# Attention and mixture of experts in one kernel: norm factors in a work bank, routing two periods sooner, token records in two tensors

## The chip, the cores and the metric

The kernel runs on one core of a Trainium2 chip. The metric is the device time of one execution in microseconds (us), lower is better. The engines are TensorE (PE, whose weight loads are listed apart as PEld), VectorE (DVE), ScalarE (ACT), GpSimd (POOL) and SyncE (SP), which here only starts transfers (DMAs).

## The reference

Eight batches of 12 heads, 448 positions, head size 64, all in float32. First attention with normalised q and k, then a mixture of eight experts beside a dense feed-forward network (FFN) on the 3584 tokens:

```python
q_n, k_n = rmsnorm(q, g_q), rmsnorm(k, g_k)        # over the 64 elements of a head
attn = softmax(q_n @ k_n.T / 8) @ v
x = attn.transpose(0, 2, 1, 3).reshape(3584, 768)  # tokens x (heads * 64)

h_dense = np.maximum(x @ w1_dense, 0.0)            # 768 -> 512
y_dense = h_dense @ w2_dense                       # 512 -> 768
logits = x @ w_gate                                # 768 -> 8
expert_idx = np.argmax(logits, axis=1)
gate_w = softmax(logits)[token, expert_idx]
for e in range(8):
    mask = expert_idx == e
    h = np.maximum(x[mask] @ w1[e], 0.0)
    y_moe[mask] = gate_w[mask, None] * (h @ w2[e])
out = y_dense + y_moe
```

## The kernel before, in words

**Attention stage.** It is cut into 24 periods `g` of four heads (two pairs of heads); three periods make a batch, `b, gb = divmod(g, 3)`. A period has seven steps `i`. In each step PE makes the scores of the next period's group for one of seven blocks of keys (`scores`, into the two double banks of PSUM pool `a_sc`), and ACT takes their exponential into SBUF (L285). In steps 1 and 2 PE multiplies the exponentials of this period with the values for the first of each pair's two heads (`attend`, head half 0, into the PSUM tile `av`), in steps 4 and 5 for the second (half 1). A column of ones beside the values gives the sums of the softmax; `divide` on DVE divides by them and writes tokens by features to `xa`.

Beside that, each period prepares later ones: `squares` (POOL) and `sums` (DVE) make the sums of squares for group g+3, `norms` (ACT: a logarithm, then two exponentials) makes the factors `rq` and `r`, `normalise` multiplies q (DVE) and k (POOL) with them into `xn`, `transposes` (PE) turns group g+2 into a work bank and `turned` (DVE) copies it out as `y`. In the kernel before, `rq` lies in unused columns of the tile `av`, and `norms` stands at the end of step 6, after `divide(g, 1)`.

**Work for the second half, woven in.** `xtrans` turns `xa` of group g-2 on PE into a work bank, `xturned` copies it to `xT` on DVE. With a whole batch in `xT`, `logits` (PE) makes the gate's logits, `choose` (DVE) picks the expert, `ranks` (PE) counts tokens per expert, `places` (DVE) finds each token's place and the selection matrices `sel`, `gates` (ACT, DVE) makes the softmax weight. `fill` gives PE dense matmuls of x with w1_dense, six in a group (`ff`), which ACT's `relu` empties. The work banks are the two banks of PSUM pool `a_wk`: each call takes the next of them, and the first instruction that writes a bank waits for the last that used it:

```python
ps = trs[name] = wkp.tile([P, J, P], BF16, tag="wk", name="tr")
R = wkp.tile([P, 512], F32, tag="wk", name="R")
ff[0] = wkp.tile([P, F], F32, tag="wk", name="ff")
```

**Records.** For each token the DRAM tensor `records` keeps 656 floats' worth: x in bf16 (384), the relu of the dense layer h (256), and the gate (16). `store` writes the parts from SP.

**The tail.** The last period (L619 to L656) is written out: attention of the last group, the rest of the routing, the rest of the dense groups, and `tables`, in which DVE works out from all counts which token lies in which slot, PE sums it up (`slp`, L448) and DVE writes the index table `row`.

**Expert stage.** The tokens are sorted into 32 to 35 tiles of 128 slots with one expert each. POOL gathers the records of a tile through `row` (`gather`, an indirect DMA, five tiles ahead). The first five tiles are turned on PE (`turn_here`, x and h apart, through one PSUM tile `xp`), later ones by transposing DMAs from SP (`turn`). Then `gemm1` (six matmuls, expert's w1), relu with the gate on ACT, `htrans`, and `gemm2`: eight matmuls of h with w2_dense and eight of the expert's w2 into the same PSUM tiles, two copies out (DVE, ACT) and an indirect DMA from POOL that scatters the tile to `out`.

The order of instructions on each engine is that of the program (`manual_schedule` over all five engines in the first half, over PE, POOL and SP in the second); engines run on their own and wait for each other through semaphores. An engine that waits holds up all that stands behind the waiting instruction.

Of the kernel before, what the change touches and what calls it, by code (L numbers as in the profile page):

```python
# [9 lines left out]
F32 = mybir.dt.float32  # L10
# [9 lines left out]
def kernel(  # L20
# [55 lines left out]
    XH = Dm // 2  # L76
    GO = XH + F // 2
    RC = GO + 16
# [21 lines left out]
    rec = nc.dram_tensor("records", (N, RC), F32).ap()  # L100
# [36 lines left out]
    def late_weight(i):  # L137

        o, w = wjobs[i]
        if i % 2:  # L140
            nc.gpsimd.dma_start(o, w, max_dma_last_dim=4 * Dm)
        else:
            nc.gpsimd.dma_start(o, w)
# [6 lines left out]
    with tc.tile_pool(name="a_ld", bufs=2) as ld, \  # L150
# [6 lines left out]


        av = avp.tile([P, GP, 512], F32, name="av")
        SP0 = 4 * De  # L160
        rq = av[:, 0, SP0:SP0 + 2 * J].rearrange("p (h j) -> p h j", h=2)
# [22 lines left out]
        gt = late[:, o:o + 8 * (RC - GO)].bitcast(F32).rearrange("p (m w) -> p m w", m=4)  # L184
        o += 8 * (RC - GO)
# [51 lines left out]
        def norms(g):  # L237
# [4 lines left out]
            rs["q"] = rq  # L242
# [88 lines left out]
        def store(b, lo, hi, x, chunks=range(4)):  # L331

            o = rec[b * S:(b + 1) * S].rearrange("(p u) w -> p u w", u=J)
            c = [m for m in chunks if m < 3]
            for hh in range(2):
                if c:
                    u = 2 * c[0] + hh
                    nc.sync.dma_start(o[:, u:u + 2 * len(c) - 1:2, lo:hi],
                                      x[hh * D:(hh + 1) * D, :len(c)])
            if 3 in chunks:  # L340
                nc.sync.dma_start(o[:, J - 1:, lo:hi], x[D:, len(c):])
# [26 lines left out]
        def gates(b, gt=gt):  # L368
# [4 lines left out]
            store(b, GO, RC, gt)  # L373
# [35 lines left out]
        def tables():  # L409
# [26 lines left out]
            slp = wkp.tile([P, NTL], F32, tag="wk", name="slp")  # L436
            for c in range(2):
# [9 lines left out]
                for n in range(c0, c1):  # L447
                    nc.tensor.matmul(slp, sel[:, n // 4, n % 4], val[:, :, n],  # L448
                                     start=(n == 0), stop=(n == NC4 - 1))

# [28 lines left out]
        def relu():  # L479
            while relus:  # L480
# [6 lines left out]
                store(b, XH, GO, hd.bitcast(F32).unsqueeze(1), [m])  # L487
# [6 lines left out]
        def period(g):  # L494
            b, gb = divmod(g, NB)
            for i in range(J):
                if i == 6:
                    divide(g, 1)
# [4 lines left out]
                if i == 0:  # L503
                    if g > 1:
                        xtrans(g - 2)
                    squares(g + 3, "k")
                    sums(g + 3, "q")
                if i == 5:
                    if gb == 0 and b > 1:
                        ranks(b - 2)  # L510
                        places(b - 2)
                    if gb == 2 and b > 0:
                        logits(b - 1)
                        choose(b - 1)
                if i in (1, 2, 4, 5):
                    for m in range(2):
                        attend(g, i // 3, (i - 1) % 3 * 2 + m)
                if i == 1:
                    if g > 1:
                        xturned(g - 2)  # L520
# [285 lines left out]
```

## Time and profile before

| | |
|---|---|
| median of 3 runs | 405.2 us (404.52 to 413.1) |
| profiled execution | 405.27 us, span 403.5 us, mean granted clock of TensorE 0.968 |
| attention stage, in the profile | 0 to about 226 us |
| tail and change of stage | about 226 to 253 us |
| expert stage | about 253 to 403 us |
| busy in the span | PE 85%, DVE 56%, ACT 54%, POOL 54% |

In a profile, a line of a timeline has the start, the time from the first start to the last end, the engine, the line of the kernel, the operation, the tiles it writes and reads with partitions x elements and type, how many instructions were merged, and in brackets how long the engine was idle before and what ended that. A part of PE's time is listed under the tile that it writes: `sc` scores, `av` attention, `tr` transposes of q and k, `xt` of x, `R` logits or ranks, `ff` dense layer, `slp` slots, `xp` turned records, `he`, `hp` and `yp` the experts. Starts are in us from the start of the span.

### The profile page before, as it was taken

The numbers are of one execution on the slowest core, as the hardware profiler recorded it, in microseconds if no ns is written. First come the engines' busy times: TensorE is split into PE (matmuls) and PEld (weight loads), VectorE is DVE, ScalarE is ACT, GpSimd is POOL, SyncE is SP. The second block draws the span as 40 slices with busy tenths as digits, with TensorE's granted clock in tenths as the row PEclk, the third lists the DMA queues.
The fourth block names the chain that finished last, engine by engine and source line by source line (L and its number), as shares of the span: only waits on it lengthen the run. The fifth ranks groups of instructions, "written<-read, shape, count | busy, mean of one in ns | idle before, by whom it ended". The sixth has DMA issues, their size and how long they took to land. (4 is left out here: it accounts for less than half of the span.)

```text
span 403.5 us, 13022 instructions
## 1 busy us (share of the span) xinstructions
PE 344.0 (85%) x5250; PEld 209.7 (52%) x5250; DVE 226.4 (56%) x554; ACT 216.4 (54%) x349; POOL 217.3 (54%) x193
## 2 busy tenths in 40 slices
PE   0688789989899898899899893799999999999990
PEld 0355565655556555555466542465555555555550
DVE  3856897887978978978786672232212121212220
ACT  4576988778788787787788321122322222222220
POOL 4896797765777676666661102534454545444220
PEclk9996999999999999999999987799999999999997
DMA  7899798959899698899672853999999999999921
GB/s 238 288 249 274 209 257 269 256 144 334 193 280 259 187 255 259 224 278 237 187 159 72 144 137 84 216 259 239 253 252 225 231 266 225 253 249 212 224 104 51
DMA packets 79372, 88.08 MB, mean 218 GB/s; under 512 B 44109, under 2 KB 71245, under 8 KB 79312
## 3 DMA queue, kind: packets, MB, share of 16 engines
q1 hardware_dynamic: 67424, 51.30, 48.9%
q0 software_dynamic: 11568, 35.93, 36.5%
q8 instruction: 44, 0.72, 0.7%
q14 instruction: 16, 0.13, 0.1%
q10 hardware_dynamic: 320, 0.00, 0.0%
HBM read 72.12 MB, written 21.99 MB: 233 GB/s over the span
## 5 line engine op out<-in xcount | busy, mean ns | idle before, releaser
L285 ACT ACTIVATE we<-sc 128x896 bf16<-128x896 f32 x168 | 147.6, 919 | 27.7 <-PE sc L282 27.1
L303 PE MATMUL av<-va,we 64*128 64x65 bf16 x2576 | 59.1, 194 | 15.9 <-DVE xn L251 13.5
L251 POOL TENSOR_TENSOR xn<-xk,r 128x896 bf16<-128x896 f32 x24 | 40.5, 1689 | 58.6 <-issue 45.5
L282 PE MATMUL sc<-y 64*64 64x448 bf16 x672 | 67.2, 392 | 4.8 <-ACT we L285 3.9
L726 DVE COPY ys<-yp 128x384 f32<-128x384 f32 x32 | 17.8, 558 | 94.8 <-issue 89.8
L728 POOL DMA_INDIRECT out_dram<-ys,dest x32 | 32.4, 1013 | 71.0 <-ACT ys L727 53.6
L303 PEld LDWEIGHTS <-we 64*128 64x128 bf16 x2688 | 51.0, 96 | 33.3 <-issue 32.2
L233 DVE TENSOR_REDUCE ssq<-sq 128x14 f32<-128x896 f32 x48 | 51.7, 1078 | 3.9 <-ACT sq L224 2.8
L668 POOL DMA_INDIRECT xg<-records,row x32 | 31.4, 982 | 33.6 <-issue 33.6
L727 ACT COPY ys<-yp 128x384 f32<-128x384 f32 x32 | 15.3, 479 | 63.4 <-PE yp L720 53.6
L693 PE MATMUL he<-we,xT 128*128 (+1 forms) x192 | 47.8, 386 | 1.2 <-issue 0.6
L698 ACT ACTIVATE hs<-he,xg 128x512 bf16<-128x512 f32 x32 | 22.0, 687 | 48.9 <-PE he L693 46.1
L474 PE MATMUL ff<-wd,xT 128*128 128x512 bf16 x192 | 47.6, 388 | 0.0
L714 PE MATMUL yp<-wd,xT 128*128 128x384 bf16 x256 | 46.8, 326 | 0.0
L720 PE MATMUL yp<-we,heT 128*128 (+1 forms) x256 | 46.8, 326 | 0.0
L226 POOL TENSOR_TENSOR sq<-xq 128x896 f32<-128x896 f32 x22 | 37.0, 1684 | 4.3 <-DMA xq<-in_q_dram 2.4
L251 DVE TENSOR_TENSOR xn<-xq,av 128x896 bf16<-128x896 f32 x24 | 26.1, 1088 | 21.8 <-ACT av L244 21.8
L226 POOL TENSOR_TENSOR sq<-xk 128x896 f32<-128x896 f32 x22 | 37.0, 1682 | 0.0
L260 PE MATMUL tr<-ident,xn 128*128 128x128 bf16 x336 | 25.9, 235 | 11.9 <-DVE xn L251 11.9
L313 DVE TENSOR_TENSOR xa<-av,inv 128x256 bf16<-128x256 f32 x92 | 34.7, 419 | 1.6
L282 PEld LDWEIGHTS <-y 64*64 64x64 bf16 x672 | 20.0, 105 | 29.2 <-issue 18.4
L714 PEld LDWEIGHTS <-xT 128*128 128x128 bf16 x256 | 24.9, 98 | 19.0
(120 smaller groups left out, 359.1 us busy)
## 6 DMA issues: line engine op xcount, KB each, us to landing
we<-in_moe_w_dram POOLq DMA_DIRECT2D x16, 768.0 KB
xq<-in_q_dram SPq DMA_DIRECT2D x24, 448.0 KB, 7.5
xk<-in_k_dram SPq DMA_DIRECT2D x24, 448.0 KB, 7.0
xv<-in_v_dram SPq DMA_DIRECT2D x24, 448.0 KB, 6.4
records<-xa SPq DMA_DIRECT2D x16, 288.0 KB, 5.0
records<-we SPq DMA_DIRECT2D x44, 64.0 KB, 3.6
wd<-in_moe_w_dense_dram POOLq DMA_DIRECT2D x2, 768.0 KB
records<-xa SPq DMA_DIRECT2D x8, 96.0 KB, 4.8
```

The source lines that it names most:

```text
L226: nc.gpsimd.tensor_mul(sqs[name, g], x, x)
L233: nc.vector.tensor_reduce(ssqs[g][:, "qk".index(name)], sqs[name, g].rearrange("p h (j d) -> p h j d", d=D), AX.X, ALU.add)
L251: (nc.vector if name == "q" else nc.gpsimd).tensor_mul(y.rearrange("p j h d -> p h j d"), xin[name, g].rearrange("p h (j d) -> p h j d", d=D),
L282: nc.tensor.matmul(ps[r * D:(r + 1) * D, hh, :S], kT[rows, r, j], qT[rows, r].rearrange("p j s -> p (j s)"), start=True, stop=True)
L285: nc.scalar.activation(x, ps[:, :, :S], AF.Exp, scale=scale)
L303: nc.tensor.matmul(avv[:, r, m], exs[g, j][rows, hh, QC[m]:QC[m] + P], va[rows, hh, j, :De], start=(j == 0), stop=(j == J - 1))
L313: nc.vector.tensor_mul(o[:, :, gb, 2 * hh:2 * hh + 2, c].rearrange("p m r d -> p r m d"), avv[:, :, :, c * D // 2:(c + 1) * D // 2], inv.t ...
L474: nc.tensor.matmul(ff[0], xTs[b][:, kk, QC[m]:QC[m] + P], wd1[:, kk], start=(kk == 0), stop=(kk == KD - 1))
L693: nc.tensor.matmul(he, xTs[t][:, kk], we[:, bass.ds(eregs[t], 1), 0, kk * F:(kk + 1) * F] .rearrange("p o f -> p (o f)"), start=(kk == 0), ...
L714: nc.tensor.matmul(yp[dd], xTs[t][:, KD + i], wd2[:, i, dd * HD:(dd + 1) * HD], start=(i == 0), stop=False)
L720: nc.tensor.matmul(yp[dd], heTs[t][:, i], we[:, bass.ds(eregs[t], 1), 1, i * Dm + dd * HD:i * Dm + (dd + 1) * HD] .rearrange("p o f -> p ( ...
L728: i = nc.gpsimd.indirect_dma_start(out=out, out_offset=bass.IndirectOffsetOnAxis(ap=dest[:, t:t + 1], axis=0), in_=ys.rearrange("p a d -> ...
```

## The change

- `norms` takes a work bank for `rq` in place of columns of `av`, and stands at the start of step 6, ahead of `divide(g, 1)`, of the relu and of the scores of that step.
- `xtrans` and `xturned` of group g-2 move from steps 0 and 1 to the end of step 2, behind the attention of half 0.
- `logits` and `choose` of a batch move from gb 2 of the next batch to gb 1; `ranks`, `places` and `gates` from gb 0 of the batch after the next to gb 2 of the next. The second dense group of a batch's periods (`fill` in step 5) moves from gb 1 to gb 0.
- The records become two tensors, `records_x` (gate and x, 400 floats) and `records_h` (256 floats), with a gather each; the first two tiles' x gathers come first, and their h parts are turned after gemm1 of tile 1.
- In the tail, the routing of the last but one batch starts at `ranks`, dense groups are spread anew (seven are left in place of six; two now come after the slot matmuls and one between their halves), `slp` takes a bank of the score pool, and every second store is issued by ACT.
- Weights of w2 from the tenth load on are loaded in smaller pieces during the periods too.

```diff
-            rs["q"] = rq
+            rq = wkp.tile([P, 512], F32, tag="wk", name="rq")[:, :2 * J]
+            rq = rs["q"] = rq.rearrange("p (h j) -> p h j", h=2)
...
+            for i, (to, of) in enumerate(dmas):
+                (nc.scalar if tail[0] and i % 2 else nc.sync).dma_start(to, of)
...
-            slp = wkp.tile([P, NTL], F32, tag="wk", name="slp")
+            slp = scp.tile([P, GP, 512], F32, tag="sc", name="slp")[:, 0, :NTL]
...
+                if c == 0:
+                    fill(NG + 1, KD)
+                    relu()
+            fill(NG + 1, 8 * KD)
+            relu()
...
             for i in range(J):
                 if i == 6:
+                    norms(g + 3)
                     divide(g, 1)
...
                 if i == 0:
-                    if g > 1:
-                        xtrans(g - 2)
                     squares(g + 3, "k")
                     sums(g + 3, "q")
                 if i == 5:
-                    if gb == 0 and b > 1:
-                        ranks(b - 2)
-                        places(b - 2)
-                    if gb == 2 and b > 0:
+                    if gb == 1 and b > 0:
                         logits(b - 1)
                         choose(b - 1)
+                    if gb == 2 and b > 0:
+                        ranks(b - 1)
+                        places(b - 1)
                 if i in (1, 2, 4, 5):
                     for m in range(2):
                         attend(g, i // 3, (i - 1) % 3 * 2 + m)
+                if i == 2 and g > 1:
+                    xtrans(g - 2)
+                    xturned(g - 2)
                 if i == 1:
-                    if g > 1:
-                        xturned(g - 2)
                     while nw[0] < len(wjobs) - LATE and (nw[0] - 2) * WPACE <= g + 1:
-                        nc.gpsimd.dma_start(*wjobs[nw[0]])
+                        (late_weight if nw[0] > 9 else nc.gpsimd.dma_start)(*wjobs[nw[0]])
...
-                if i == 5 and gb == 1:
+                if i == 5 and gb == 0:
                     fill(g, KD)
                 if i == 6:
-                    norms(g + 3)
                     normalise(g + 3, "q")
                     normalise(g + 3, "k")
                     if gb == 2:
-                        store(b, 0, XH, xas[b].bitcast(F32))
-                    if gb == 0 and b > 1:
-                        gates(b - 2)
+                        store(b, XO, HO, xas[b].bitcast(F32))
+                        if b > 0:
+                            gates(b - 1)
                     load_v(g + 4)
                     fill(g, KD)
...
                 xtrans(g - 2)
-                logits(B - 2)
                 for hh in range(2):
                     for m in range(4):
                         attend(g, hh, m)
                     if hh == 0:
                         xturned(g - 2)
-                        choose(B - 2)
                         xtrans(g - 1)
+                ranks(B - 2)
                 relu()
                 divide(g, 0)
                 xturned(g - 1)
-                ranks(B - 2)
                 divide(g, 1)
-                store(B - 1, 0, XH, xas[B - 1].bitcast(F32))
+                store(B - 1, XO, HO, xas[B - 1].bitcast(F32))
+                fill(g, 4)
                 xtrans(g)
                 places(B - 2, (0, 1))
+                fill(g, 2)
                 xturned(g)
-                places(B - 2, (2,))
+                places(B - 2, (2, 3))
                 logits(B - 1)
+                relu()
+                gates(B - 2, gts[0])
+                choose(B - 1)
                 fill(g, KD)
-                choose(B - 1)
                 relu()
-                places(B - 2, (3,))
                 ranks(B - 1)
-                gates(B - 2, gts[0])
                 gates(B - 1, gts[1])
-                fill(NG + 1, 8 * KD)
+                fill(NG + 1, 2 * KD)
                 relu()
                 tables()
...
-        def gather(t):
-            xg = sb.tile([P, RC], F32, tag="xg", name="xg", bufs=7)
+        def gather(t, part):
+
+            if part == 0:
+                xgs[t] = sb.tile([P, RC], F32, tag="xg", name="xg", bufs=7)
             nc.gpsimd.indirect_dma_start(
-                out=xg, out_offset=None, in_=rec,
+                out=xgs[t][:, HO:] if part else xgs[t][:, :HO], out_offset=None, in_=recs[part],
                 in_offset=bass.IndirectOffsetOnAxis(ap=row[:, t:t + 1], axis=0))
...
+            for t in range(t0, min(t0 + 2, t1)):
+                gather(t, 0)
             for t in range(t0, min(t0 + ahead, t1)):
-                gather(t)
+                if t > t0 + 1:
+                    gather(t, 0)
+                gather(t, 1)
...
             turn_here(t0, 0)
-            turn_here(t0, 1)
             gemm1(t0)
-            for n in range(2 if t0 + 1 < t1 else 0):
-                turn_here(t0 + 1, n)
+            if t0 + 1 < t1:
+                turn_here(t0 + 1, 0)
             htrans(t0)
             for t in range(t0, t1):
                 if t + ahead < t1:
-                    gather(t + ahead)
+                    gather(t + ahead, 0)
+                    gather(t + ahead, 1)
                     turn(t + ahead)
                 if t + 1 < t1:
                     gemm1(t + 1)
+                if t == t0:
+                    for i in range(t0, min(t0 + 2, t1)):
+                        turn_here(i, 1)
```

## The prediction

> **What bounds the kernel now.** I read the page first (busy shares, the 40 slices), then busy time by stage, then the order of time on TensorE (PE), VectorE (DVE) and GpSimd (POOL) in one batch and at the change of stage. The chain of waits ends in the closing 2 us and tells nothing here.
>
> ```profile
> span 403.5 us, 13022 instructions
> PE   0688789989899898899899893799999999999990
> 99.00:126.00 27.00, 24.42 (x543) 15.35 (x542) 23.12 (x57) 21.66 (x36) 19.21 (x14) 1.00 0.92 242
> 245.30:253.00 7.70, 0.00 (x0) 0.03 (x1) 1.64 (x8) 0.00 (x0) 2.99 (x3) 0.65 0.38 88
> 300.00:350.00 50.00, 50.00 (x316) 28.81 (x315) 10.66 (x24) 14.06 (x25) 24.35 (x25) 1.00 1.06 238
> ```
> Columns of the stage rows: window, length, busy us of PE, weight load, DVE, ACT, POOL, granted clock, DMA share, GB/s. Attention is held by PE (24.4 of 27.0 us per batch) with DVE right behind (23.1), so a wait of one for the other shows at once. The expert stage is PE without a gap. Between them PE does nothing for 7.7 us.
>
> ```profile
> 160.82 0.18 PE L383 MATMUL R<-oh,tri 128*128 128x32 bf16 x1 [0.28 <-DVE y L268]
> 161.64 0.38 PE L282 MATMUL sc<-y 64*64 64x448 bf16 x4
> 161.96 1.47 PE L474 MATMUL ff<-wd,xT 128*128 128x512 bf16 x6
> 165.90 0.62 PE L303 MATMUL av<-va,we 64*128 64x65 bf16 x28 [1.29 <-DVE xn L251]
> ...
> 161.22 0.16 DVE L392 TENSOR_TENSOR counts<-R,counts 128x8 f32<-128x8 f32 x1
> 162.78 0.76 DVE L406 TENSOR_SCALAR sel<-iop,R 128x128 f16<-128x128 bf16 x4
> 164.76 1.09 DVE L251 TENSOR_TENSOR xn<-xq,av 128x896 bf16<-128x896 f32 x1 [0.31 <-ACT av L244]
> ```
> A period of gb 0. The ranks in R stay on DVE until `sel` ends at 163.54, while PE went from R to the dense matmuls `ff` after 1.14 us: `ff` had the other work bank. What PE pays is 1.29 us later, where attention waits for `xn`, whose factors lie in the bank of `av`.
>
> ```profile
> 235.82 7.40 PE L474 MATMUL ff<-wd,xT 128*128 128x512 bf16 x30
> 243.06 2.14 PE L448 MATMUL slp<-val,sel 128*128 128x35 f16 x32
> 253.00 0.80 PE L686 MATMUL xp<-ident,xg 128*128 128x128 bf16 x6 [7.79 <-DMA xg<-records,row]
> ...
> 249.18 1.06 POOL L668 DMA_INDIRECT xg<-records,row  x1 [24.13 <-issue]
> ...
> 245.93 0.55 SPq L341 DMA_DIRECT2D records<-hd  x1
> ```
> The last dense work runs under the routing tables on DVE. The slot matmuls end at 245.2, the last store of h is issued at 245.93, the first gather starts 3.25 us after that, PE resumes 3.8 us later.
>
> [...] The 1.29 and 0.49 us before `av` recur every batch; it is the same kind of gap that I expect elsewhere. [...] small stores of h here landed after 2.0 us median.
>
> **The change part by part.** Start-to-start prices from the timelines of 152 to 209: four score matmuls (sc) 0.315, 28 attention matmuls (att) 0.545, xt 0.55, 14 transposes 0.89, six dense (ff) 1.40, logits 0.68, ranks 0.28. A batch is 21 sc, 12 att, 3 xt, 3 transposes, 4 ff, logits, ranks: 6.6+6.5+1.65+2.7+5.6+0.7+0.3 = 24.0 us of PE. Before it takes 26.95 (exps at 99.00 and 125.95), so 2.95 of stalls.
>
> *Norms in a work bank.* It removes `av` <- `xn`: 13.5 us over 14 waits, 1.8 to 2.3 a batch. But each period now takes six tiles from the two work banks, not five: xt A, q-transposes B, k-transposes A, then B for R or the extra ff, A for rq, and B again for the last ff. Before, that ff took the bank of the k-transposes, long free. The order of the changed program says so too: the last ff follows, and waits for, DVE (gb 1: `choose`; gb 2: the fourth `sel`) or ACT (gb 0: the relu of the first ff). It blocks PE: the next scores stand behind it.
>
> *xt moved from step 0 to step 2, after the attention of head half 0.* Time from the first sc of a period. Step 0 has nothing to hide exp: sc of step 2 waits for the first exp, 0.43+0.92+0.05 = 1.40 against 1.18 when PE is ready: 0.22. att to 2.26, xt to 2.88, its copy on DVE from 2.94 (0.53); only then divide (0.24+0.67), so att of half 1 waits 0.15; then sums 1.0 and y from 5.38 to 6.06. Before, divide began at 2.76 and R at 5.41 (160.82 less 155.41). Now R, which needs y's bank, starts at 6.11; PE is ready at 5.36: 0.75.
>
> Then the last ff:
> - gb 1: logits 6.11; mx 0.79 later, oh ends 1.40 after that: 8.30; PE is ready at 7.65: 0.7. Period 9.76.
> - gb 2: ranks 6.11; counts at 6.55 (0.39 later, and behind y), 2.34 to the end of `sel`: 8.9; PE ready at 7.25: 1.7. Period 10.35.
> - gb 0: the extra ff waits 0.2 for y, the last ff 0.45 for a relu of 0.60 (less one sc). Period 9.67.
>
> Batch: 29.8, +2.85. The first sc of period 4 to the end of the loop: before 54.97 to 225.79 = 170.8. After: five batches 148.9, then 9.76 and 10.35, and two periods without norms and loads (9.0, 7.4; before 8.1, 8.25): 185.4. **+14.6.** If DVE or the banks are half as late: +7; if PE also repeats the pause of 1.05 us at 153.36 without cover: +16.
> Periods 0 to 3 have no dense work; period 1 loses its 1.16 wait at a slow clock, 2 and 3 come to 7.3 as before (exp bound): -0.5 (-2 to 0).
>
> *Tail.* From PE's xt at 225.79 (=0); before, the gather is at 23.4. Routing of the last-but-one batch is shorter, but `logits` now stands behind `places` and waits for `sel` to 7.0 (PE idle 1.7). choose ends 9.2, ranks 9.25. On ACT a store issue (0.6) stands before the gates' exp, so counts is at 11.0, against 10.97 before: nothing gained. counts to val 4.75; slots 15.8 to 16.85, an ff to 18.2, slots to 19.3, two ff to 22.1, relu 22.8, store and landing 3.25: gather at 26.1, **+2.7**. The point is that the gather of x doesn't get away from the stores of h[...]. Bounds: -4 (gather at the row table, 19.8) to +4.
> *Start of the experts.* x alone brings gemm1 of tile 0 forward by 0.95, but three turns with one `xp` bank stand between gemm1(1) and gemm2(0), each with a copy of 0.42 to 0.56 that PE waits out: gemm1(1) 9.2, itself 1.46, two turns of 0.4 with a copy of 0.5, a turn 0.5, gemm2 1.46+0.39+1.46, htrans 0.38 put gemm1(2) at 16.7 after the gather, before 15.45: **+1.25** (-1 to +2).
> *Two gathers a tile.* POOL per tile: 1.01+0.30+0.98+0.30+0.98 = 3.57 of 4.12 us: fits. h is 1.28 later, transposes likewise; they are issued 5.8 to 9.7 us ahead of their gemm1 and land after 5.1 median, so most still fit; tile 30 already waits 0.6. **+0.5** (0 to 6).
> *Late weights in smaller pieces, two queues for the last stores*: same bytes, 0 (-0.5 to +0.5); the issue leaves SP, which had a queue of seven stores, and enters ACT.
>
> Sum against the profiled execution, 405.3 (span 403.5 and 1.8 around it; median of the runs 405.2): 405.3+14.6-0.5+2.7+1.25+0.5 = 423.85, taken as 424.
>
> **Rivals.**
> 1. *Forecast, the work banks and the later DVE chain stall PE*: 424, own range 414 to 431. Chance 0.80. For it: the chain is made of measured pieces, and its rules applied to the period at 155.41 give R and ff where the trace has them.
> 2. *The same, and the experts become bound by DMA or POOL.* The DMA share is 1.06 there; twice as many indirect transfers, 0.2 us more a tile for 27 tiles: 424+6 = 430, up to 436. Chance 0.07. Against: no lead of the transposes is seen to shrink over the stage.
> 3. *A draw.* DVE gets ahead where ACT no longer holds it (its waits for rq were 21.8 us), half of the new stalls vanish: +7 and +1: 411. Chance 0.08. Against: DVE's lateness now comes from xt, not from ACT.
> 4. *Faster: the removed wait for `xn` is all that counts.* Place: the last ff of a period. It decides if that ff finds its bank free within 0.1 us, so that a batch costs 24.0 and 1.1 of small stalls: 25.1, -1.85 for six batches = -11; with a gather of x that starts with the row table, -4: 405.3-15 = 390. Chance 0.05. Against: the waits of the ff and of the first gather that the program's order shows.
>
> **Numbers.** 424; range 411 to 433. A difference under about 2% can't be told from none here: slower by over 2% (above 413.4) 0.87, within 0.08, faster 0.05.
>
> **What would show it.** Right: no wait `av` <- `xn`; new ones before ff, on DVE `sel`/`oh` and ACT, near 0.7, 1.7 and 0.45 us; R waits 0.75 for y; batches near 29.8; the first gather 3 us after the last store of h; tiles at 4.12. Wrong: batches under 27.5, or a gather of x that starts while `ff` runs.

## The result, and the profile after

The changed kernel took 465.1 us (median of 4; three between 464.0 and 465.4, one 472.5) against 406.3 us for the kernel before (median of 4): ratio 1.146 (1.138 to 1.153). Some executions of a kernel take over 1.5% longer than its fastest, mostly at a lower granted clock; the ratios leave them out, the medians do not, and the table of experiments has a – where the profile is of one. Its profiled execution has a span of 462.3 us against 403.5, so 58.8 us are to be explained; the forecast had 18.55. Split as the forecast was:

| stretch | before | after | difference | forecast |
|---|---|---|---|---|
| start to PE's `xt` that opens the tail | 225.8 | 274.1 | +48.3 | +14.1 |
| from there to the first gather | 23.4 | 29.9 | +6.5 | +2.7 |
| first gather to the end | 154.3 | 158.3 | +4.0 | +1.75 |

First the page: its header, PE's row in 40 slices and the granted clock in tenths; below them the clock's row of before. Before, PE was busy at 0.8 or more in 17 of the first 20 slices, and the clock was at 0.9 or more in all slices but five.

```profile
span 462.3 us, 13041 instructions
PE   1597785984985984985886985638989999999991
PEclk9997997997987988887898889765999999999996
...
PEclk9996999999999999999999987799999999999997
```

After, PE dips once in every three slices, a batch's length, and the clock dips beside it. The waits of PE (engine, line waited for: us in total, times, longest) say at what; the last line is the wait of before that the change was to remove:

```profile
PE ff L482 <- DVE sel L409: 27.0, 6, 5.2
...
PE slp L451 <- DVE val L446: 5.3, 1, 5.3
PE R L386 <- DVE y L267: 3.9, 6, 0.7
PE R L351 <- DVE y L267: 3.9, 6, 0.7
PE ff L482 <- DVE oh L368: 3.2, 5, 0.6
...
PE ff L482 <- ACT we L493: 1.9, 5, 0.4
...
PE av L303 <- DVE xn L251: 13.5, 14, 1.3
```

`av` <- `xn` is gone. The new waits are the ones forecast: R for y 0.65 (forecast 0.75), `ff` for `oh` 0.64 (0.7), for the relu on ACT 0.37 (0.45). One is not its size: `ff` for `sel` waits 4.3 to 5.2 us in five of six periods and 2.9 in the last, not 1.7. A period of gb 2 on PE, DVE and POOL, from the timelines (start, length, what, idle before it and until what); the last two lines are POOL before, around the `sel` of 162.78 to 163.54 that the prediction shows:

```profile
106.39 0.18 PE L386 MATMUL R<-oh,tri 128*128 128x32 bf16 x1 [0.65 <-DVE y L267]
112.76 0.61 PE L482 MATMUL ff<-wd,xT 128*128 128x512 bf16 x1 [5.17 <-DVE sel L409]
113.59 1.91 PE L482 MATMUL ff<-wd,xT 128*128 128x512 bf16 x4 [0.22 <-issue]
115.43 0.96 PE L281 MATMUL sc<-y 64*64 64x448 bf16 x8
...
108.35 4.35 DVE L409 TENSOR_SCALAR sel<-iop,R 128x128 f16<-128x128 bf16 x4
...
107.42 1.69 POOL L250 TENSOR_TENSOR xn<-xk,r 128x896 bf16<-128x896 f32 x1 [3.79 <-PE av L302]
109.06 1.68 POOL L224 TENSOR_TENSOR sq<-xk 128x896 f32<-128x896 f32 x1
110.68 0.80 POOL L530 DMA_DIRECT2D we<-in_moe_w_dram  x1
111.48 0.98 POOL L212 CAST va<-xv 128x896 bf16<-128x896 f32 x1
...
160.57 1.69 POOL L226 TENSOR_TENSOR sq<-xq 128x896 f32<-128x896 f32 x1
164.99 1.69 POOL L251 TENSOR_TENSOR xn<-xk,r 128x896 bf16<-128x896 f32 x1 [2.73 <-issue]
```

The chain up to `sel` is on time: counts 0.4 us after R, `sel` starts at 108.35. But the four `sel` then take 4.35 us where the same four took 0.76 before. POOL is busy without a gap from 107.42 to 112.46, because the earlier norms brought its `xn` and what follows it to this place; before, POOL was idle from 162.26 to 164.99, while `sel` ran. One by one, the first three `sel` end at 109.15, 110.79 and 112.53, each 0.05 to 0.06 us after an item of POOL ends (109.10, 110.74, 112.47); the fourth takes 0.25.

After that wait the granted clock is 0.50. The table by stretch (length, busy us of PE, weight load, DVE, ACT, POOL, granted clock, DMA share, GB/s) has the matmuls after that pause, those after the two short waits of a gb 1 period, and the last dense groups in the tail:

```profile
112.76:115.70 2.94, 2.72 (x9) 0.92 (x14) 2.87 (x7) 0.00 (x0) 0.00 (x0) 0.50 0.94 162
133.65:136.90 3.25, 3.10 (x13) 0.85 (x14) 2.93 (x6) 0.55 (x2) 3.25 (x4) 0.55 0.09 33
291.40:299.70 8.30, 7.97 (x49) 4.18 (x49) 3.13 (x14) 1.26 (x3) 0.00 (x0) 0.61 0.06 16
```

In the tail the counts are late, because ScalarE's exp of the last gates stands behind a store in ScalarE's own queue, and the wait in front of it, 2.39 us, ends with the landing of an earlier store:

```profile
282.99 0.60 ACT L493 ACTIVATE hd<-ff 128x512 bf16<-128x512 f32 x1 [2.28 <-PE ff L482]
285.48 0.45 ACTq L344 DMA_DIRECT2D records_h<-hd  x1
285.98 0.23 ACT L372 ACTIVATE eg<-eg 128x32 f32<-128x32 f32 x1 [2.39 <-DMA records_x<-xa]
...
303.96 1.05 POOL L677 DMA_INDIRECT xg<-records_x,row  x1 [30.57 <-issue]
```

The expert stage is PE without a gap, as before: from 350 to 440 us PE is busy 89.4 of 90.0 us, and a tile takes 4.12 us.

### The profile page after: what moved, and what is told of

It reads as the page before. It is cut to its first block, busy times and chain, and to the rows that moved or that the text cites. A ratio compares the mean times of both kernels' runs of the same rounds, so it can differ in the third digit from the quotient of the medians.

```text
span 462.3 us, 13041 instructions
## 1 busy us (share of the span) xinstructions
PE 362.4 (78%) x5213; PEld 216.8 (47%) x5250; DVE 242.4 (52%) x554; ACT 218.5 (47%) x349; POOL 247.6 (54%) x225
## 4 chain that ended last, share of the span: by engine, by line
PE 53%; DVE 23%; DMA 8%; ACT 6%; issue 5%; SPq 2%; POOL 1%; POOLq 0%; ACTq 0%; DVEq 0%
PE ff L482 9%; PE he L701 9%; PE yp L722 8%; PE yp L728 8%; PE sc L281 5%; PE av L302 5%; DVE sel L409 5%; DVE ssq L231 4%; ACT we L284 4%; DVE xa L312 4%; DMA records_x<-xa 2%; PE xt L322 2%; DVE y L267 2%; PE tr L259 2%; DVE xT L328 2%
## 5 line engine op out<-in xcount | busy, mean ns | idle before, releaser
L482 PE MATMUL ff<-wd,xT 128*128 128x512 bf16 x170 | 57.5, 461 | 35.5 <-DVE sel L409 27.0
L302 PEld LDWEIGHTS <-we 64*128 64x128 bf16 x2688 | 52.2, 98 | 27.1 <-issue 26.2
L302 PE MATMUL av<-va,we 64*128 64x65 bf16 x2576 | 60.5, 196 | 4.4 <-issue 3.1
L677 POOL DMA_INDIRECT xg<-records_x,row x32 | 31.2, 976 | 40.0 <-issue 39.7
L701 PE MATMUL he<-we,xT 128*128 (+1 forms) x177 | 46.1, 396 | 3.7 <-DMA xT<-xg 1.5
L722 PE MATMUL yp<-wd,xT 128*128 128x384 bf16 x256 | 48.1, 332 | 0.0
L482 PEld LDWEIGHTS <-xT 128*128 128x128 bf16 x192 | 19.7, 111 | 59.8 <-DVE sel L409 28.6
L328 DVE COPY xT<-xt 128x896 bf16<-128x896 bf16 x24 | 15.0, 624 | 56.1 <-PE xt L322 56.1
L259 PE MATMUL tr<-ident,xn 128*128 128x128 bf16 x336 | 27.1, 234 | 11.6 <-DVE xn L250 11.6
L677 POOL DMA_INDIRECT xg<-records_h,row x32 | 30.3, 947 | 10.6 <-issue 9.5
```

Source lines behind the costliest of these rows:

```text
L259: nc.tensor.transpose(ps[:, j], xn[name, g][:, j].rearrange("p h d -> p (h d)"), ident)
L302: nc.tensor.matmul(avv[:, r, m], exs[g, j][rows, hh, QC[m]:QC[m] + P], va[rows, hh, j, :De], start=(j == 0), stop=(j == J - 1))
L482: nc.tensor.matmul(ff[0], xTs[b][:, kk, QC[m]:QC[m] + P], wd1[:, kk], start=(kk == 0), stop=(kk == KD - 1))
L677: nc.gpsimd.indirect_dma_start(out=xgs[t][:, HO:] if part else xgs[t][:, :HO], out_offset=None, in_=recs[part], in_offset=bass.IndirectOff ...
L701: nc.tensor.matmul(he, xTs[t][:, kk], we[:, bass.ds(eregs[t], 1), 0, kk * F:(kk + 1) * F] .rearrange("p o f -> p (o f)"), start=(kk == 0), ...
L722: nc.tensor.matmul(yp[dd], xTs[t][:, KD + i], wd2[:, i, dd * HD:(dd + 1) * HD], start=(i == 0), stop=False)
```

## The experiments

The runs are to be read with one thing in mind, the chip. The kernel before took 406 to 407 us on every chip, but kernels with two gathers a tile did not take the same on all. So the table has the chip's number (those of the first two rows are not known, nor whether it is one chip), the start of the tail ("loop"), the time from there to the first gather ("tail"), and from there to the end ("experts"), all from the profile.

| kernel | chip | median us | ratio to before (95%) | loop | tail | experts |
|---|---|---|---|---|---|---|
| before | first | 406.3 | 1 | 225.8 | 23.4 | 154.3 |
| after | first | 465.1 | 1.146 (1.138 to 1.153) | 274.1 | 29.9 | 158.3 |
| sel_from_psum | 8 | 458.0 | 1.128 (1.122 to 1.135) | 245.7 | 30.6 | 179.5 |
| norms_late | 8 | 459.3 | 1.129 (1.122 to 1.135) | 248.3 | 30.4 | 179.8 |
| rq_in_sbuf | 8 | 471.9 | 1.158 (1.152 to 1.164) | 259.5 | 31.2 | 179.9 |
| stores_on_sp | 8 | 478.1 | 1.176 (1.170 to 1.182) | 270.6 | 24.8 | 177.5 |
| after_again | 6 | 486.9 | 1.202 (1.193 to 1.211) | 270.6 | 30.9 | 181.9 |
| sel_psum_one_record | 6 | 432.5 | 1.066 (1.057 to 1.075) | 246.3 | 30.2 | 154.0 |
| before_split_records | 6 | 429.2 | 1.059 (1.049 to 1.070) | 225.6 | 23.4 | 177.8 |
| before_q_on_gpsimd | 6 | 430.9 | 1.066 (1.054 to 1.078) | 246.8 | 23.4 | 154.8 |
| three_undone | 12 | 427.6 | 1.048 (1.038 to 1.057) | 245.3 | 24.7 | 152.1 |
| three_undone_xt_back | 12 | 411.5 | 1.011 (1.002 to 1.019) | 229.8 | 25.5 | 152.0 |
| before_rq_sbuf | 12 | 417.6 | 1.021 (1.013 to 1.030) | – | – | – |
| before_q_on_gpsimd_2 | 12 | 401.8 | 0.986 (0.978 to 0.994) | 222.5 | 23.5 | 154.0 |
| after_chip_three | 14 | 466.0 | 1.150 (1.143 to 1.156) | 271.8 | 28.7 | 163.5 |
| split_old_order | 14 | 412.6 | 1.018 (1.012 to 1.024) | 225.2 | 22.9 | 162.1 |
| one_more_gather | 14 | 416.2 | 1.016 (1.007 to 1.026) | – | – | – |
| q_on_gpsimd_again | 14 | 404.3 | 0.992 (0.989 to 0.995) | 220.8 | 24.0 | 154.1 |

**What stretches `sel`.** Theory: GpSimd's elementwise work, from 107.42 to 112.46 us in after, holds up VectorE's `sel` beside it. Rival: the bank, or VectorE's own queue. Three kernels, each with one edit to after.

```diff
# sel_from_psum
-                for m in range(4):
-                    nc.vector.tensor_scalar(sel[:, b, m], iop, lof[:, m:m + 1], None,
-                                            op0=ALU.is_equal)
+                nc.vector.tensor_tensor(sel[:, b], iop.unsqueeze(1).to_broadcast([P, 4, P]),
+                                        lof.unsqueeze(2).to_broadcast([P, 4, P]), ALU.is_equal)
# norms_late
-                    norms(g + 3)            # ahead of divide(g, 1)
+                    norms(g + 3)            # ahead of normalise(g + 3, "q"), as before
# rq_in_sbuf
-            rq = wkp.tile([P, 512], F32, tag="wk", name="rq")[:, :2 * J]
-            rq = rs["q"] = rq.rearrange("p (h j) -> p h j", h=2)
+            rq = rs["q"] = sb.tile([P, 2, J], F32, tag="rq", name="rq")
```

> The kernel after, with one edit: the four `sel` comparisons of a batch (each with two plain operands in SBUF) become one tensor_tensor instruction of 4x128 elements whose second operand is the place in PSUM. Norms, banks, routing and records stay as they are. Theory (VectorE's `sel` is held up by GpSimd's elementwise work that the earlier norms bring beside it): `sel` takes about 0.6 us once instead of up to 4.35, the dense matmul of gb 2 waits about 1.5 us instead of 4.3 to 5.2, a gb 2 period falls from a mean of 14.8 us to about 10.4, and the time from 465 to about 438 (430 to 444). Rival (the stretch lies in the bank of R, in the low clock after the pause or in VectorE's own queue, not in GpSimd): `sel` takes as long in one piece as it did in four, and the time stays within 1% of 465.

> The kernel after, with one edit: the norms are issued where they were before the change, behind the divide and the scores of step 6, so that GpSimd's normalising of k starts 1 to 2 us later; rq stays in the work bank. Theory (GpSimd beside `sel`): `sel` starts before GpSimd's work and takes about 0.8 to 1.2 us for four, the dense matmul of gb 2 waits about 2 us, a gb 2 period takes about 11 us, and the time is about 442 (434 to 452). Rival (the bank alone): `sel` and its wait keep their size, and the time stays within 1% of 465.

> The kernel after, with one edit: the norms rq are a small tile in SBUF, not in a work bank. So five tiles a period take the two work banks, as before the change, and the last dense matmul of a period takes the bank of the transposes of k. Theory (the bank makes PE wait, GpSimd makes the wait long): no wait of the dense matmuls for `sel` or `oh` is left, `sel` itself stays stretched to about 4 us for four, so VectorE is late instead, with up to 1.7 us more where xn of q, now with two operands in SBUF, meets GpSimd; a gb 2 period falls from 14.8 to about 11, gb 1 from 10.4 to about 9, and the time to about 433 (422 to 445). Rival (VectorE's chain bounds the period by itself, whatever bank the dense matmuls have): the wait moves to attention's divide or the turned transposes at the same size, and the time stays above 455.

The answers on `sel` by line (count, then duration in ns, minimum/median/maximum), of after, of norms_late and of sel_from_psum, and PE's wait in the last:

```profile
L409 DVE TENSOR_SCALAR sel<-iop,R x24: 245/805/1825, 74.1 to 251.9; 128x128 f16<-128x128 bf16 x24
...
L409 DVE TENSOR_SCALAR sel<-iop,R x24: 250/251/259, 73.6 to 227.1; 128x128 f16<-128x128 bf16 x24
...
L408 DVE TENSOR_TENSOR sel<-iop,R x6: 686/686/686, 72.6 to 225.0; 128x512 f16<-128x512 bf16 x6
...
PE ff L481 <- DVE sel L408: 9.0, 6, 1.5
```

Two different edits give the same. With GpSimd's `xn` 1.8 us later, behind `sel`, the very instruction that took 805 ns takes 251 again. As one tensor_tensor `sel` takes 0.69 us although GpSimd's `xn` runs beside it as in after. What this edit changes is the form of the instruction: the place lies in PSUM both times (`sel<-iop,R` in both lines), so the old form did not have two operands in SBUF, as the expectation says. PE's wait falls from 5.2 to 1.5 us (the forecast had 1.7), a gb 2 period (from its first scores to those of the next) from a mean of 14.6 to 10.5, with norms_late to 10.9, and the loop from 271 to 274 us (the runs of after) to 246 and 248. The theory stands, its rival falls. The totals did not follow (458 and 459, not 438 and 442), since the expert stage of these runs took 21 us more: see below.

rq_in_sbuf was a miss: 472 and not 433, and the expert stage explains only 21 of these 39 us. The dense matmuls' waits for `sel` and `oh` are gone, but `sel` stays stretched, and now the normalising of q, with two operands in SBUF, is stretched as well (1.61 us in the median and up to 4.18, in after 1.08). What its rival named came too: attention waits for `divide` (`xa`) instead, 21.5 us in place of 27.0:

```profile
L249 DVE TENSOR_TENSOR xn<-xq,rq x24: 1081/1614/4177, 9.0 to 241.7; 128x896 bf16<-128x896 f32 x24
...
PE av L301 <- DVE xa L311: 21.5, 7, 4.1
```

So the bank sets which of PE's instructions waits; that it waits for 5 us is GpSimd's doing. Freeing the bank (with the new stretch of q's normalising in it) brought the loop to 259.5, ending the collision alone to 245.7.

**The tail's two queues.**

```diff
# stores_on_sp (edit to after)
-                (nc.scalar if tail[0] and i % 2 else nc.sync).dma_start(to, of)
+                nc.sync.dma_start(to, of)
```

> The kernel after, with one edit: the stores of the tail are all issued by SP, none by ACT. Theory (a store in ACT's queue[...] holds up the exp of the last gates, VectorE waits 3.1 us for it): counts come about 1.5 us sooner after the start of the tail, the first gather about 1.5 us sooner, and the time is about 463.5 (ratio to the kernel after 0.994 to 0.998). Rival (SP's queue of 8 stores then ends later than the last relu): the first gather comes no sooner or up to 2 us later, and the time is 465 to 467.

Direction right, size wrong: the first gather comes 24.8 us after the start of the tail, not 29.9. ScalarE's `eg` of the last gates starts at once, PE's pause ahead of the slots is 2.84 us instead of 5.28, and its clock stays up. PE at the slots (in after: 5.28 us idle before them), and the stretch of the last dense groups:

```profile
285.50 1.15 PE L451 MATMUL slp<-val,sel 128*128 128x35 f16 x16 [2.84 <-DVE val L446]
...
287.90:291.50 3.60, 3.60 (x29) 1.95 (x26) 1.69 (x8) 1.20 (x2) 0.00 (x0) 1.00 0.30 71
```

Clock 1.00 where after had 0.61: of the 5.1 us, 2.4 is the shorter pause, the rest the dense groups at full speed. The three profiles of after have 28.7 to 30.9 us here, so the gain is 4 to 6 us; three_undone below has 24.7, on a third chip. The total (478, above the 465 of after) can't be compared across chips; against after_again on chip 6 the whole run is shorter too.

**The expert stage.** All four kernels above have after's code in it, and took 177 to 180 us there, after 158. Next:

> The kernel after, unchanged, beside the other runs of this call on one chip. In its first profile the expert stage took 158 us from the first gather to the end; in the four variants of it that ran since it took 177 to 180 us, though none touched that stage. Theory 1 (the expert stage with two gathers a tile has two rhythms, and which one it takes hangs on small things ahead of it): after keeps its own, 463 to 467. Theory 2 (the chip of that run made the difference): on this chip after too shows about 179 us from the first gather to the end, and takes about 486.

```diff
# sel_psum_one_record: sel_from_psum, with one tensor and one gather a tile, slots() in the order of before
-    recs = [nc.dram_tensor("records_x", (N, HO), F32).ap(),
-            nc.dram_tensor("records_h", (N, RC - HO), F32).ap()]
+    rec = nc.dram_tensor("records", (N, RC), F32).ap()
# before_split_records: before, with the two tensors, store(), gather() and slots() of after
```

> The kernel sel_from_psum (after, with `sel` as one instruction), with the split of the records undone: one tensor of records, one gather a tile, gathers and turns in the order of before; the order of the fields and the two queues of the last stores stay. sel_from_psum took 179 us from its first gather to the end. Theory (two gathers a tile bring the slow rhythm of the expert stage): with one gather PE is the bound again, 154 us from the first gather to the end as in before, so 458 less 25: about 433 (427 to 439). Rival (the slow rhythm comes from something else): it stays at 452 or more.

> The kernel before, with the split alone: records of x and of h in two tensors, two gathers a tile, the gathers and turns in the order of after; all stores on SP; attention, norms and routing as before. The forecast priced this at 1.25 for the start and 0.5 for the rest: about 407 to 409. Theory of the slow rhythm (two gathers a tile): the expert stage takes 177 to 180 us from the first gather instead of 154, and the time is about 429 (424 to 434).

All three came out at their theory's figure: 487 (486), 432.5 (433), 429.2 (429). So on chip 6 the split costs 23 us of the expert stage by itself and 28 behind the rest of the change, and with one gather the stage takes 154 us again. The stretch of the expert stage, in before_split_records and in sel_psum_one_record:

```profile
300.00:400.00 100.00, 85.08 (x517) 47.93 (x518) 17.95 (x41) 22.56 (x41) 58.77 (x60) 1.00 0.86 199
...
320.00:420.00 100.00, 100.00 (x635) 57.81 (x633) 22.13 (x50) 28.45 (x49) 43.84 (x44) 1.00 1.01 228
```

PE is idle 15 of 100 us, while the DMA share falls to 0.86: the stage isn't bound by the amount that DMA moves. In sel_from_psum every second tile shows it (PE, DVE):

```profile
364.09 1.46 PE L727 MATMUL yp<-we,heT 128*128 x8
370.08 1.46 PE L727 MATMUL yp<-we,heT 128*128 x8 [1.71 <-DVE heT L714]
...
369.04 0.56 DVE L733 COPY ys<-yp 128x384 f32<-128x384 f32 x1 [7.06 <-issue]
369.51 0.41 DVE L714 COPY heT<-hp 128x512 bf16<-128x512 bf16 x1
```

The matmuls end at 365.5, the copy of their result on DVE starts at 369.04 (on ACT at 369.06), and the turned h, next on DVE, is what PE then waits for. In the records it is the signal that comes late: the matmuls that end at 365.39, 365.55, 365.77, 367.07 and 368.37 add to PE's semaphore in one bunch, at 368.96 to 369.22, while in the trace of after each such addition comes within 0.02 us of its matmul's end (384 to 393 us). All six profiles with 177 us or more have such bunches (37 to 44% of PE's additions come within 0.12 us of the one before, 1% or less in every other profile). What holds the signals up stays open. These six profiles also lack most records of landings (6 for a transfer, against 9 to 11 with one gather on chips 6 and 12, and 16 in the profiles of after and of chip 14), so the recording may have a part in it; no run tests that. Three runs ask whether the chip, the order or the number of transfers makes it.

```diff
# split_old_order: before_split_records, with slots() of before, both gathers of a tile together
# one_more_gather: before, with one indirect gather more a tile
+            nc.gpsimd.indirect_dma_start(
+                out=sb.tile([P, D], F32, tag="xe", name="xe", bufs=7), out_offset=None,
+                in_=q.rearrange("b h s d -> (b h s) d"),
+                in_offset=bass.IndirectOffsetOnAxis(ap=row[:, t:t + 1], axis=0))
```

> The kernel after, unchanged, on one more chip. Theory (the slow rhythm of the expert stage is the usual one with two gathers a tile, the first profile the exception): about 180 us from the first gather to the end, 484 to 488 us. Rival (it is as likely as not, by the chip): 463 to 467.

> The kernel before_split_records with the gathers and turns in the order of before (both gathers of a tile together, the turns of x and h together): the split alone, without the new order at the start of the experts. Theory (two gathers a tile keep GpSimd at 3.85 us of 4.12 per tile, and the stage can't get back what a late transfer costs): the slow rhythm stays, 425 to 432 us. Rival (the order at the start sets the rhythm): 405 to 411.

> The kernel before with one indirect gather more a tile, of 256 bytes a row from q into a tile that nothing reads; records, their one gather and all orders as in before. Theory 1 (the number of indirect transfers that GpSimd issues brings the slow rhythm): as with the split, 424 to 432 us. Theory 2 (it comes from the two tensors, or from the waits of x, h and their turns for each other): 405 to 411.

On chip 14 after takes 466 again, with 163.5 us of experts. So it goes by the chip, or by the time at which each was used, which no run tells apart: with two gathers it takes 4 to 9.5 us more in the first result and on chip 14, 23 to 28 on chips 6 and 8, while one gather gives 152 to 155 us in all seven rows of the table that have it. My theory that the slow rhythm is the usual one, and the first profile the exception, is wrong. On chip 14 the split in the old order still costs 7 us in all, so the new order at the start is not needed for that; and a gather of 256 bytes a row that nothing reads costs as much as the split (ratios 1.016 and 1.018; both missed the ranges of both theories). So one more indirect transfer a tile is enough for this cost, without two tensors; of one_more_gather only two executions count, and neither kernel ran on a chip with the large cost. With two gathers POOL has three issues of 1.28 us a tile, 3.85 us of 4.12. That this lack of slack is the mechanism is argued only. In before_split_records, at 5.1 us a tile, POOL itself waits 2.8 us at every second one, so it isn't full there; and what differs between the chips stays open.

**What is left: the place of xt.**

```diff
# three_undone: sel_psum_one_record with the tail's stores on SP
# three_undone_xt_back: and
                 if i == 0:
+                    if g > 1:
+                        xtrans(g - 2)
-                if i == 2 and g > 1:
-                    xtrans(g - 2)
-                    xturned(g - 2)
                 if i == 1:
+                    if g > 1:
+                        xturned(g - 2)
```

> The kernel sel_psum_one_record (after with `sel` as one instruction and with one tensor of records) with the tail's stores all issued by SP. Against 432.5 us for that kernel. Theory (ScalarE's stores hold up the last gates, and TensorE's clock drops in the pause that follows): the first gather comes about 25 us after the start of the tail instead of 30, and the time is 425 to 428. Rival (the gain seen with two tensors of records does not add to the other two): 431 to 434. What is left against before (about 407) is then the norms in a work bank and the place of xt, with the earlier routing: about 19 us, near the 14.1 of the forecast for the attention stage.

> The kernel three_undone with xt and its copy back at steps 0 and 1 of a period; norms stay in a work bank, the routing stays sooner. Theory of the forecast (the turned transposes are late because the copy of xt now stands ahead of the first divide, so R and what follows it comes 0.7 us later): R without its wait of 0.65, the score matmuls of step 2 without 0.28, periods of about 9.05, 9.5 and 8.95 us for gb 1, 2 and 0 instead of 9.73, 10.19 and 9.62, 0.7 us in each of 20 periods: 13 to 14 us less than three_undone, so about 412. Rival (the bank that the norms take makes the last dense matmul wait, wherever xt stands): PE's wait moves into that matmul and the time falls by less than 5 us.

Both theories met: 427.6 and 411.5. Putting xt back takes 15.5 us out of the loop. PE's waits in the loop, with xt back:

```profile
PE ff L480 <- DVE sel L407: 9.0, 6, 1.5
PE ff L480 <- DVE oh L367: 2.8, 5, 0.6
PE ff L480 <- ACT we L491: 1.9, 5, 0.4
PE R L385 <- DVE y L266: 1.7, 6, 0.3
```

R waits 0.3 instead of 0.65 us; the scores waited for ACT once instead of 18 times. The waits for the bank of R are as large as ever: 13.7 us, about what the removed wait for `xn` cost (13.5). The norms in a work bank are thus close to an even trade; with the sooner routing they leave the loop 4.0 us longer than before.

**Is there a version that wins?** The aim was to free `av` from `xn`. Two ways without a work bank, both with `sel` in one instruction:

```diff
# before_rq_sbuf: before, and
-            rs["q"] = rq                                     # columns of av
+            rq = rs["q"] = sb.tile([P, 2, J], F32, tag="rq", name="rq")
# before_q_on_gpsimd: also
-            (nc.vector if name == "q" else nc.gpsimd).tensor_mul(
+            nc.gpsimd.tensor_mul(
# before_q_on_gpsimd_2: instead of the last
+            (nc.vector if name == "q" and g < 3 else nc.gpsimd).tensor_mul(
# and sums(g + 3, "k") moved from ahead of turned() to behind it
```

> The kernel before, with two edits that aim at the wait which the change set out to remove, without its price: the normalising of q moves from VectorE to GpSimd, so that its factors can lie in a small SBUF tile[...] and neither a work bank nor the bank of `av` is needed; and `sel` is one instruction with its second operand in PSUM. Theory: attention's waits for `xn` (13.5 us in all) and ScalarE's for `xa` go, VectorE is lighter by 1.08 us a period, GpSimd goes from 19 to about 24 of 27 us a batch: batches of about 25.3 us instead of 26.95, and about 395 in all (389 to 401). Rival (GpSimd, with 3.4 us behind the norms before the transposes can start, is late): PE waits for `xn` at the transposes instead, 404 to 415.

> The kernel before with two edits: the factors of q in a small SBUF tile of their own, so that neither attention nor a work bank waits for them, and `sel` as one instruction with its place in PSUM. VectorE still normalises q, now with two operands in SBUF beside GpSimd. In the variant of after with rq in SBUF that instruction took 1.61 us in the median and up to 4.18, not 1.08. Theory 1 (VectorE starts first, since its factors are ready 0.2 us before those of k, and GpSimd waits): no wait of attention for `xn`, batches of about 25.5 us, 394 to 400. Theory 2 (GpSimd's squares of the period before still run, VectorE waits for them): up to 1 us lost per period on VectorE, which is busy 23 of 27 us: 405 to 415.

> The kernel before_q_on_gpsimd with two edits: the first three periods normalise q on VectorE (there PE waited up to 11 us for GpSimd), and the sums of k stand behind the turned transposes on VectorE, not ahead of them (there VectorE waited 1.6 to 1.7 us a period for GpSimd's squares, and R for VectorE). Theory: the start is that of before, R waits no more, and batches take about 26 us: 396 to 404. Rival (GpSimd itself is the bound with 8.6 us of work a period and a wait for the norms in each): periods of 9.5 us and more, 412 or above.

> The kernel before_q_on_gpsimd_2, unchanged, in more rounds and on another chip. It took 401.8 us against 407.2 of before there (ratio 0.978 to 0.994). Expected again: a ratio of 0.983 to 0.990.

The first failed as its rival said, though at 431 beyond its range: PE waited up to 11 us for GpSimd in the first periods, and VectorE for GpSimd's squares, R for VectorE:

```profile
105.77 0.74 PE L346 MATMUL R<-wgb,xT 128*128 128x8 bf16 x24 [1.61 <-DVE y L266]
...
104.04 1.09 DVE L231 TENSOR_REDUCE ssq<-sq 128x14 f32<-128x896 f32 x1 [1.74 <-POOL sq L224]
```

before_rq_sbuf came out on theory 2's side, at 417.6 just beyond its range. before_q_on_gpsimd_2 took both faults away and is faster than before, by under 2%: 401.8 us, ratio 0.986. On another chip, in 22 executions, it was 404.3, ratio 0.992 (0.989 to 0.995), just outside the 0.983 to 0.990 expected; one of the 22 took 1725 us, which no record explains. So a version without that wait gained 3 to 6 us net, with q's normalising on GpSimd, and not by way of the banks. That it is the lighter VectorE that brings this is argued: its edits were not tried one by one.

## Why the prediction was right or wrong

*The direction, and the mechanism of the forecast.* Right: the loop is held by the work banks and the later chain on VectorE. With the stretched `sel` out of it (sel_from_psum, three_undone) and the clock at full speed, the forecast's period lengths are what the traces show most often: gb 1 9.73 (forecast 9.76), gb 2 10.19 (10.35), gb 0 9.62 us (9.67). In after, periods 0 to 3 are as before (first scores of period 4 at 55.03 against 54.97; forecast -0.5). In three_undone the loop is 19.5 us longer than before where 14.1 were forecast; five of its periods still take 11.0 to 11.6 us, and one of them has a stretch near half clock (0.55 from 92.0 to 95.4 us).

*"2.34 to the end of `sel`".* This is the step that failed. The 2.34 came from the period at 160.82, where POOL stood idle. After, the part with `sel` takes 4.35 instead of 0.76 us. The prediction moved the norms and followed their effect on banks and on PE, but not on POOL, whose `xn` and squares move with them to the very place of `sel`. Six gb 2 periods at a mean of 14.6 instead of 10.35 us are 25.5 of the 34.2 us that the loop exceeded its forecast. What the runs show of the cause: the first three `sel` end with POOL's items, as above; with POOL's `xn` behind them the four take 0.25 us each (norms_late); and the one tensor_tensor takes 0.69 us under the same POOL work. Why POOL's work stretches the tensor_scalar and not this tensor_tensor, no trace shows.

*PE's clock.* Not in the sum at all. After the six waits for `sel` it is 0.50 for 2.8 to 5.1 us of PE's time, and six dense matmuls then take 2.67 us (112.76 to 115.43) instead of 1.38 (123.93 to 125.31, clock 1.00). Around the wait shown above, PE's last matmul ends at 107.59, the clock is at half from 110.10 on, 2.5 us later, PE resumes at 112.76, and the clock is full again from 116.95 on, 4.2 us after that. What brings it down is not shown. In three of six gb 1 periods the matmuls are as slow (0.55 in the row above) after waits of only 0.65 and 0.64 us with 1.6 us of work between, which makes these periods 0.6 to 1.3 us longer than 9.73. That is some 2.9 us of the loop, 1.5 more in period 22 (from its xt to the next one 7.50 us, 5.95 in other runs), and 2.7 in the tail.

*"Two queues for the last stores ... 0 (-0.5 to +0.5)".* Wrong: 5.1 us (4 to 6 by the other profiles of after). The prediction itself says that the issue "enters ACT" and put a store ahead of the gates' exp, but priced the issue (0.6), not the wait for an earlier store to land (ScalarE's `eg` waits 2.39 us). Without ScalarE's stores the tail costs +1.4 (forecast +2.7). The first gather of x starts 3.2 us after the last store of h is issued (300.8 to 303.96 in after; 3.25 before), as forecast.

*"Two gathers a tile ... +0.5 (0 to 6)".* In the first result within its bounds with the start (together +4.0, forecast 1.75); on chips 6 and 8 23 to 28 us, far outside. Rival 2 had a slower expert stage ("bound by DMA or POOL"), but put it at 6 us, at most 12, and what binds the stage stays open. The figure of 3.57 for POOL left out 0.28 of issue a tile; it is 3.85.

*The other rivals.* The draw (411) and the faster case (390) are out: the latter would have needed an `ff` that finds its bank free within 0.1 us. The signs to look for were right, except 1.7 for `sel` and batches of 29.8, which are near 35.

Added up for the first result: the forecast's 18.55, 25.5 for `sel`, about 8.7 for the rest of the loop (half of it the clock, the other half not traced to a cause), 3.8 for the tail and 2.25 for the experts give 58.8.

## What to carry to other kernels

When an instruction is moved, follow what it releases on every engine, and ask what will then run at the same time as what: two engines that never met before may hold each other up. Here no wait in the trace shows it, only that four `sel` take 4.35 us beside POOL's work instead of 0.76. Read a duration off a trace together with what the neighbour engine did at that moment. A store in the queue of an engine that also computes can cost it far more than the issue (here 0.45 us), namely the wait until an earlier store has landed (2.39 us). And a change that adds transfers to a stage is to be measured on more than one chip (here 158 to 182 us for one stage of one program).

## What was not expected of the hardware

- The same program, after with its two gathers a tile, takes 158 us in its expert stage in the first result, 164 on chip 14 and 182 on chip 6; with one gather the stage takes 152 to 155, on chips 14 and 6 too.
- In the 177 to 182 us form, VectorE's and ScalarE's copies start together 3.5 us after the matmuls that they wait for (365.5 to 369.04); PE's signals are recorded late and in bunches (five at 368.96 to 369.22).
- TensorE's granted clock fell to 0.55 over 3.25 us after two waits of 0.65 us, 1.6 us apart, in half of the gb 1 periods, and not in the others.
- GpSimd is held up as well: in rq_in_sbuf six of its 24 `xn` of k took 2.43 to 2.48 us instead of 1.69, the six beside which VectorE's `xn` of q had started first.
